# Feature products of an attention layer summed in PSUM by two matmuls of 128 columns, with maxima and exponentials taken straight from PSUM

## The chip, the cores and the metric

The kernel runs on one core of a Trainium2 chip. The metric is the device time of one execution in microseconds (us). Before the change it is 1089.97 us, the median of three runs (1088.09 to 1090.83).

## The reference

The kernel computes a linear attention with random features, followed by a two-layer network with ELU. Cut to what matters:

```python
q_s, k_s = q * scale, k * scale                   # 8 batches x 8 heads, 576 tokens, 64 wide; scale = 64 ** -0.25
def phi(x):
    proj = einsum('bhsd,md->bhsm', x, omega)      # 128 features
    h = proj - sum(x * x, -1, keepdims=True) / 2
    return exp(h - max(h, -1, keepdims=True)) / sqrt(m)
q_p, k_p = phi(q_s), phi(k_s)
kv, z = einsum('bhsm,bhsd->bhmd', k_p, v), sum(k_p, axis=2)
attn = einsum('bhsm,bhmd->bhsd', q_p, kv) / (einsum('bhsm,bhm->bhs', q_p, z)[..., None] + 1e-6)
x = attn.transpose(0, 2, 1, 3).reshape(4608, 512)
return elu(x @ w_in) @ w_out                      # 512 -> 2048 -> 512
```

The change is inside `phi`.

## The kernel before, in words

Two heads make a pair; 32 pairs are worked on one after the other (`pair`, L653). For each pair the kernel loads k, q and v, projects k to features (`project`, L394), forms kv and z (`kv`, L521), projects q, and finishes the division and the product with kv (`finish`, L558). The result lands in a ring of tokens, from which the network reads blocks of 384 tokens: a first layer (`layer1`, L751: matmuls L764 to L766 into the tile ph) and a second (`layer2`, L789: matmuls L798 to L800 into acc). Each of these products is written as three matmuls of type fp32r on a number's head (rounded to fp32r) and its tail (the rest): head by head, head by tail, tail by head.

`project` has two branches. The first pairs (k of pairs 0 to 6, q of pairs 0 to 7) take the branch `native`, with plain fp32 matmuls (L437), a maximum straight from PSUM (L445) and exponentials straight from PSUM (L404). All later ones, 25 projections of k and 24 of q, take the branch below it, which the change rewrites. There a projection has 9 slots of 128 tokens by 128 features:

- x's own tokens are squared on ScalarE (ACT, L457) and summed on VectorE (DVE, L460) into sq, nine numbers per partition.
- y holds x's head in one half of the 128 partitions and its tail in the other (L469 to L477). om holds omega's head in columns 0 to 127 and omega's tail in columns 128 to 255.
- For each slot one matmul of type fp32r with 256 columns (L488), with y stationary and om moving, gives two products of 128 columns side by side. Five chunks of two slots (the last has one) each take a PSUM bank with the tag "pa", of which there are three.
- ACT reads the second product and makes p2 = sq - product (L497). DVE subtracts p2 from the first product, writes h to SBUF and takes its maximum, in one instruction per slot (L506, which the trace shows with a short second one that reads the accumulator).
- ACT negates the maxima (L410) and takes the exponentials of h in SBUF with them as the bias (L404), one instruction per slot, in groups of four and five slots.

The order of the work is set before anything runs. Every step is entered into a plan (`Plan`, L96) with an engine, a cost in nanoseconds and a due time; `Plan.order` goes through a made-up time line with these costs and starts, on each free engine, the ready step that is due first, if its buffers are free. What comes out is a fixed order of instructions for each engine. On the chip every engine follows its list and waits on semaphores. The plan's cost of a matmul is in `mm` (L264). Batches 2 to 7, the pairs 8 to 31, are spread over the network's steps on earlier tokens, so on TensorE (PE) the matmuls of a projection stand between those of the two layers.

Of the kernel before, what the change touches and what calls it, by code (L numbers as in the profile page):

```python
# [18 lines left out]
P = 128  # L19
# [40 lines left out]
CONV_STEP = -0.51  # L60
CONV2 = 0.84
CONV3 = 70.47


SPLIT = (0, 8, 16)
# [30 lines left out]
class Plan:  # L96
# [19 lines left out]
    def op(self, eng, ns, due, fn, reads=(), writes=(), nbytes=0, alt=None):  # L116
        n = len(self.tasks)
        engs = {eng: (ns, 0.0)}
        for e, *t in alt or ():
            engs[e] = tuple(t)  # L120
        f = fn if alt is not None else lambda e: fn()
        deps, bufs = set(), set()
        for k in reads:
            if k in self.writer:
                deps.add(self.writer[k])
            self.readers.setdefault(k, []).append(n)
        for k in writes:
            if k in self.writer:
                deps.add(self.writer[k])
            deps.update(self.readers.pop(k, ()))  # L130
            self.writer[k] = n
        for k in (*reads, *writes):
            b = k[0] if isinstance(k, tuple) else k
            if isinstance(b, Buf):
                bufs.add(b)
        deps.discard(n)
        for b in bufs:
            b.left += 1
        self.tasks.append((engs, due, f, deps, bufs, nbytes))
# [123 lines left out]

def mm(n, m=1):  # L264

    return m * (n / 2.4 + 2.5)


def act(n, psum=False, ptr=False):
    return (51 if psum else 93) + 0.833 * n + (93 if ptr else 0)  # L270


def dve(n, fast=False):
    return 69 + n / (1.92 if fast else 0.96)
# [7 lines left out]
def performer_elu_kernel(  # L282
# [82 lines left out]
    def native(i, what):  # L365
        return i < NNAT[what]

    def bank(i, early, name):

        tag = early if i < NEARLY else "pa"  # L370
        return Buf(ps, [P, 512], F32, tag, name, dict(pa=3, ph=2).get(tag, 1))
# [22 lines left out]
    def project(i, nm, due):  # L394

        s = st[i]
        x = s["x" + nm]
        h = s["h" + nm] = Buf(sb, [P, NJ, M], F32, "h", f"h{nm}_{i}", 4)
        mx, nb = small("mx" + nm, NJ, f"mx{nm}_{i}"), small("nb" + nm, NJ, f"nb{nm}_{i}")

        def exps(g, js, src, due, reads):
            def f():
                for j in js:
                    nc.scalar.activation(  # L404
                        h()[:, j, :], src(j), AF.Exp, bias=nb()[:, j:j + 1], scale=SCALE
                    )
            op("ACT", len(js) * act(M, native(i, nm), True), due, f, (*reads, (nb, g)), ((h, g),))

        def negate(g, js, due):
            op("ACT", act(4), due, lambda: nc.scalar.mul(nb()[:, js], mx()[:, js], -SCALE), ((mx, g),), ((nb, g),))  # L410

        if native(i, nm):
            for a in range(2):
                def square(e, a=a):
                    if e == "ACT":
                        nc.scalar.activation(x()[D:P, a], x()[0:D, a], AF.Square)
                    else:
                        tt(e, x()[D:P, a], x()[0:D, a], x()[0:D, a], ALU.mult)

                op(  # L420
                    "ACT", act(S), due - 3 + a, square, ((x, a),), ((x, a, 2),),
                    alt=other("sq", "POOL", pool(S), "DVE", dve(S)),
                )
            for g in range(3):
                d = due + 2.2 * g
                p = bank(i, "acc%d" % g, f"pp{nm}_{i}_{g}")
                n = 4 if g < 2 else 1
                js = slice(4 * g, 4 * g + n)

                def mms(g=g, p=p):  # L430
                    for c in range(4 if g < 2 else 2):
                        t, a = 2 * g + c // 2, c % 2
                        if g < 2:
                            o = p()[:, c * M:(c + 1) * M]
                        else:
                            o = p()[a * D:a * D + D, 0:M]
                        nc.tensor.matmul(o, x()[:, a, t * P:min(t * P + P, S)], of, start=True, stop=True)  # L437

                def view(p=p):
                    return p().rearrange("p (j x) -> p j x", j=4)  # L440

                op("PE", 872 if g < 2 else 240, d, mms, [*((x, a, 2) for a in range(2)), "of"], (p,))
                op(
                    "DVE", 66 + n * 133, d + 1,
                    lambda js=js, n=n, view=view: nc.vector.tensor_reduce(mx()[:, js], view()[:, 0:n], AX.X, ALU.max),  # L445
                    (p,), ((mx, g),),
                )
                negate(g, js, d + 1.1)
                exps(g, range(js.start, js.stop), lambda j, g=g, view=view: view()[:, j - 4 * g], d + 1.5, (p,))
            return  # L450

        def t():
            return x()[:, 1].rearrange("p (j d) -> p j d", d=D)

        op(
            "ACT", act(S), due - 4,
            lambda: nc.scalar.activation(t(), t(), AF.Square, scale=(SCALE * 0.5) ** 0.5), ((x, 3),), ((x, 3),),  # L457
        )
        sq = small("sq" + nm, NJ, f"sq{nm}_{i}")
        op("DVE", dve(S), due - 3, lambda: nc.vector.tensor_reduce(sq(), t(), AX.X, ALU.add), ((x, 3),), (sq,))  # L460

        y = Buf(sb, [P, 2 * S], F32R, "t", f"t{nm}_{i}", 2)
        for a in range(2):
            r, o = slice(a * D, a * D + D), slice(D - a * D, P - a * D)
            cs = slice(a * S, a * S + S)
            parts = ((x, 0),)
            op(  # L469
                "ACT", act(S), due - 5 + a, lambda e, r=r, cs=cs: copy(e, y()[r, cs], x()[r, 0]), parts, ((y, a, "h"),),  # L470
                alt=other("y_hi", "DVE", dve(S, True)),
            )
            op(
                "POOL", pool(S), due - 4 + a,
                lambda e, r=r, o=o, cs=cs: tt(e, y()[o, cs], x()[r, 0], y()[r, cs].bitcast(F32), ALU.subtract),
                (*parts, (y, a, "h")), ((y, a, "l"),), alt=other("y_lo", "DVE", dve(S)),
            )  # L477
        for c in range(5):
            d = due + 1.1 * c
            p = Buf(ps, [P, 512], F32, "pa", f"pp{nm}_{i}_{c}", 3)  # L480
            p2 = Buf(sb, [P, 2, M], F32, "p2", f"p2{nm}_{i}_{c}", 2)
            n = 2 if c < 4 else 1
            g = 0 if c < 2 else 1

            def mms(c=c, p=p, n=n):
                for a in range(n):
                    o = a * (S + D) + c * P
                    nc.tensor.matmul(p()[:, a * 256:(a + 1) * 256], y()[:, o:o + P], om, start=True, stop=True)  # L488

            def view(p=p):  # L490
                return p().rearrange("p (a x) -> p a x", a=2)

            op("PE", mm(256, n), d, mms, [(y, a, z) for a in range(2) for z in "hl"] + ["oh", "om"], (p,))
            def rest(c=c, n=n, p2=p2, view=view):
                for a in range(n):
                    j = 2 * c + a
                    nc.scalar.activation(  # L497
                        p2()[:, a], view()[:, a, M:], AF.Identity, bias=sq()[:, j:j + 1], scale=-1.0
                    )

            op("ACT", n * act(M, True, True), d + 0.5, rest, (p, sq), (p2,))

            def ttr(c=c, n=n, p2=p2, view=view):
                for a in range(n):
                    j = 2 * c + a
                    nc.vector.tensor_tensor_reduce(  # L506
                        out=h()[:, j, :], in0=view()[:, a, 0:M], in1=p2()[:, a, :], scale=1.0, scalar=LOWEST,
                        op0=ALU.subtract, op1=ALU.max, accum_out=mx()[:, j:j + 1],
                    )

            op("DVE", n * 212, d + 1, ttr, (p, p2), ((h, g, c), (mx, g)))
            if c in (1, 4):
                js = range(0, 4) if c == 1 else range(4, NJ)
                negate(g, slice(js.start, js.stop), d + 1.1)
                exps(g, js, lambda j: h()[:, j, :], d + 1.5, [(h, g, e) for e in range(5)])

    def parts_of(i, nm):
        h = st[i]["h" + nm]
        return [(h, g) for g in range(3 if native(i, nm) else 2)]

    def kv(i, due):  # L521

# [35 lines left out]
    def finish(i, due):  # L558
# [15 lines left out]
        for g in range(3):  # L574
# [3 lines left out]
            slots = [(j, j % 2, slice(0, P)) for j in range(4 * g, 4 * g + 4)]  # L578
            if g == 2:
                slots = [(8, a, slice(a * D, a * D + D)) for a in range(2)]  # L580
            hg = (h, g) if native(i, "q") else (h, min(g, 1))

            def dens(slots=slots):
                for j, a, r in slots:
# [365 lines left out]
```

## Time and profile before

| | before |
|---|---|
| median of three runs | 1089.97 us |
| span of the profiled execution | 1090.7 us |
| TensorE's mean granted clock, share of full speed | 0.987 |
| TensorE matmul records | 5971, busy 97% of the span |
| DVE busy, ACT busy, GpSimd (POOL) busy | 58%, 66%, 37% |
| DMA, mean rate | 162 GB/s |

A record of a matmul holds its way through the array too, so records overlap each other: a matmul of 384 columns is shown as 338 to 348 ns long while the next one starts 0.17 us after it. What a matmul costs TensorE is therefore read from the start of one to the start of the next, and not from its length. "PE" are the matmuls, "PEld" the loads of the stationary operand. A plain fp32 matmul shows as two records, each with a weight load of its own; an fp32r matmul shows as one. The rows of a timeline give the start in us, the time to the end of the last record, the engine, the line, the operation, out<-in, the shapes and the number of records.

### The profile page before, as it was taken

To read this page: it belongs to the slowest core of one execution; us is meant where nothing else is said; L and a number is where in the kernel's file an instruction comes from. 1 tells how busy PE (TensorE), PEld (TensorE's weight loads), DVE (VectorE), ACT (ScalarE), POOL (GpSimd) and SP (SyncE) were. 2 spreads that over 40 slices of the span, in tenths; PEclk is the share of its full clock that TensorE was granted. 3 is DMA by queue.
4 is the path that set the end of the run, shared out by engine and by line. 5 is a ranking of instruction groups with operands and counts; after the bars stand their busy time and mean duration, and the time that the engine had idled before them with its cause. 6 is when DMAs were issued, how large, how long until landed. Compare 5 with 4: busy or idle time off the path is not lost.

```text
span 1090.7 us, 19072 instructions
## 1 busy us (share of the span) xinstructions
PE 1060.6 (97%) x5971; PEld 936.8 (86%) x5971; DVE 635.9 (58%) x2403; ACT 724.7 (66%) x2027; POOL 404.4 (37%) x372
## 2 busy tenths in 40 slices
PE   7979888999999999999999999999999999999998
PEld 7867777889988888999888888899888888899987
DVE  6788988775776775225676666324566775322221
ACT  6878774546988986337888988326888888432222
POOL 3568746661223343222343233322233342222221
PEclk8889998999999999999999999999999999999999
DMA  7554656656663554434554645434444452343431
GB/s 213 171 181 161 208 188 240 218 186 205 207 205 130 169 170 150 165 118 157 176 155 153 193 139 170 162 119 150 162 155 167 157 164 79 117 164 119 161 121 63
DMA packets 53235, 176.90 MB, mean 162 GB/s; under 512 B 6032, under 2 KB 6224, under 8 KB 53136
## 3 DMA queue, kind: packets, MB, share of 16 engines
q1 hardware_dynamic: 53136, 175.69, 48.4%
q8 instruction: 48, 0.79, 0.3%
q14 instruction: 51, 0.42, 0.1%
HBM read 155.48 MB, written 20.19 MB: 161 GB/s over the span
## 4 chain that ended last, share of the span: by engine, by line
PE 79%; DVE 9%; ACT 6%; issue 3%; DMA 1%; POOL 1%; SPq 0%; DVEq 0%; POOLq 0%; ACTq 0%
PE ph L764 11%; PE acc L798 10%; PE acc L800 10%; PE ph L766 10%; PE acc L799 10%; PE ph L765 10%; PE pkv L535 4%; PE ppq L488 3%; PE pn L634 3%; PE pt L607 2%; PE ppk L488 2%; ACT hk L404 1%; DVE u_w L697 1%; DVE u_w L704 1%; DVE u_w L709 1%
## 5 line engine op out<-in xcount | busy, mean ns | idle before, releaser
L336 POOL TENSOR_TENSOR g<-e,g 128x384 fp32r<-128x384 f32 x182 | 189.2, 1040 | 547.7 <-DVE g L333 405.9
L764 PE MATMUL ph<-xh,w1c 128*128 128x384 f32 x768 | 267.5, 348 | 6.7 <-DVE e L777 6.2
L766 PE MATMUL ph<-xh,w1c 128*128 128x384 f32 x768 | 259.8, 338 | 0.0
L765 PE MATMUL ph<-xl,w1c 128*128 128x384 f32 x768 | 259.7, 338 | 0.0
L777 DVE SCALAR_TENSOR_TENSOR e<-e,ph 128x384 f32<-128x384 f32 x192 | 105.9, 552 | 237.2 <-ACT e L774 232.8
L798 PE MATMUL acc<-w2h,g 128*128 128x512 f32 x576 | 231.4, 402 | 0.0
L773 ACT ACTIVATE e<-ph 128x384 f32<-128x384 f32 x192 | 93.6, 488 | 206.4 <-PE ph L766 198.4
L800 PE MATMUL acc<-w2h,g 128*128 128x512 f32 x576 | 227.7, 395 | 0.0
L799 PE MATMUL acc<-w2l,g 128*128 128x512 f32 x576 | 227.4, 395 | 0.0
L764 PEld LDWEIGHTS ph<-xh,w1c 128*128 128x128 f32 x768 | 145.6, 190 | 20.1 <-DVE e L777 8.5
L765 PEld LDWEIGHTS ph<-xl,w1c 128*128 128x128 f32 x768 | 145.8, 190 | 7.2
L766 PEld LDWEIGHTS ph<-xh,w1c 128*128 128x128 f32 x768 | 145.4, 189 | 0.3 <-POOL w1c L336 0.3
L800 PEld LDWEIGHTS acc<-w2h,g 128*128 128x128 f32 x576 | 108.5, 188 | 25.5
L798 PEld LDWEIGHTS acc<-w2h,g 128*128 128x128 f32 x576 | 108.7, 189 | 15.1 <-issue 2.3
L799 PEld LDWEIGHTS acc<-w2l,g 128*128 128x128 f32 x576 | 108.8, 189 | 12.2
L336 POOL TENSOR_TENSOR hq<-hq,den 128x512 f32<-128x512 f32 (+1 forms) x96 | 90.4, 961 | 36.1 <-DVE den L595 24.6
L774 ACT ACTIVATE e<-e 128x384 f32<-128x384 f32 x192 | 100.7, 525 | 3.1
L333 DVE CAST g<-e 128x384 fp32r<-128x384 f32 x166 | 72.8, 439 | 23.5 <-PE acc L800 18.8
L586 DVE CUSTOM_DVE_ANT_0 junk<-hq,pz 128x128 f32<-128x128 f32 (+1 forms) x320 | 74.1, 279 | 16.9 <-PE pz L570 16.1
L506 DVE CUSTOM_DVE_ANT_0 hq<-ppq,p2q 128x128 f32<-128x128 f32 x216 | 54.3, 287 | 41.8 <-ACT p2q L497 40.2
L506 DVE CUSTOM_DVE_ANT_0 hk<-ppk,p2k 128x128 f32<-128x128 f32 x225 | 56.5, 286 | 36.1 <-ACT p2k L497 34.3
L497 ACT ACTIVATE p2q<-ppq,sqq 128x128 f32<-128x128 f32 x216 | 67.8, 367 | 12.5 <-PE ppq L488 10.8
(82 smaller groups left out, 1620.3 us busy)
## 6 DMA issues: line engine op xcount, KB each, us to landing
w1c<-w1s SPq DMA_DIRECT2D x176, 512.0 KB, 3.3
raw_w<-in_w_dram SPq DMA_DIRECT2D x32, 512.0 KB, 3.6
xk<-in_kx_dram SPq DMA_DIRECT2D x25, 576.0 KB, 3.9
xq<-in_qx_dram SPq DMA_DIRECT2D x24, 576.0 KB, 4.6
v<-in_v_dram SPq DMA_DIRECT2D x32, 325.0 KB, 3.4
out_dram<-o SPq DMA_DIRECT2D x36, 256.0 KB, 2.9
w1s<-w1c SPq DMA_DIRECT2D x16, 512.0 KB, 3.2
xq<-in_q_dram SPq DMA_DIRECT2D x8, 288.0 KB, 4.0
```

Source lines behind the costliest of these rows:

```text
L336: (nc.vector if e == "DVE" else nc.gpsimd).tensor_tensor(*args)
L506: nc.vector.tensor_tensor_reduce(out=h()[:, j, :], in0=view()[:, a, 0:M], in1=p2()[:, a, :], scale=1.0, scalar=LOWEST, op0=ALU.subtract, o ...
L586: nc.vector.tensor_tensor_reduce(out=junk()[r], in0=h()[r, j, :], in1=pz()[r, a * P:(a + 1) * P], scale=1.0, scalar=EPS, op0=ALU.mult, op1 ...
L764: nc.tensor.matmul(ph(), wh, xh[:, c, o:o + TB], start=(c == 0), stop=False)
L765: nc.tensor.matmul(ph(), wh, xl[:, c, o:o + TB], start=False, stop=False)
L766: nc.tensor.matmul(ph(), wl, xh[:, c, o:o + TB], start=False, stop=(c == NC - 1))
L773: op("ACT", act(TB, True), due, lambda: nc.scalar.activation(e(), ph(), AF.Relu, scale=-1.0), (p,), (e,))
L774: op("ACT", act(TB), due + 0.2, lambda: nc.scalar.activation(e(), e(), AF.Exp, scale=-1.0), (e,), (e,))
L777: lambda: nc.vector.scalar_tensor_tensor(e(), e(), -1.0, ph(), ALU.add, ALU.max), (p, e), (e,),
L798: nc.tensor.matmul(a(), g()[:, 0, ts], w2h[:, f], start=(f == f0), stop=False)
L799: nc.tensor.matmul(a(), g()[:, 0, ts], w2l[:, f], start=False, stop=False)
L800: nc.tensor.matmul(a(), g()[:, 1, ts], w2h[:, f], start=False, stop=(f == f1 - 1))
```

## The change

In the second branch of `project` the two products of a slot are no longer written side by side but added up in the same 128 columns of PSUM by two matmuls of 128 columns, one with omega's head and one with its tail as the moving operand, both with the same stationary y. Four slots share a bank, so a projection has three groups (4, 4 and 1 slots). The maximum of a group is one DVE instruction on PSUM. sq, which now carries the square of the scale, goes into the bias by two small DVE instructions per group, and the exponentials read PSUM. p2, the ACT steps L497 and L410 of this branch and the DVE step L506 are gone. The divisor in the plan's cost of a matmul gets a name with its value unchanged.

```diff
-            op("ACT", len(js) * act(M, native(i, nm), True), due, f, (*reads, (nb, g)), ((h, g),))
+            op("ACT", len(js) * act(M, True, True), due, f, (*reads, (nb, g)), ((h, g),))
...
-            lambda: nc.scalar.activation(t(), t(), AF.Square, scale=(SCALE * 0.5) ** 0.5), ((x, 3),), ((x, 3),),
+            lambda: nc.scalar.activation(t(), t(), AF.Square, scale=SCALE * 0.5**0.5), ((x, 3),), ((x, 3),),
...
+        def bias(g, js, due):
+            def f():
+                nc.vector.scalar_tensor_tensor(mx()[:, js], mx()[:, js], SCALE, sq()[:, js], ALU.mult, ALU.subtract)
+                nc.vector.scalar_tensor_tensor(nb()[:, js], mx()[:, js], -1.0, sq()[:, js], ALU.mult, ALU.subtract)
+            op("DVE", 2 * dve(4), due, f, ((mx, g), sq), ((mx, g), (nb, g)))
...
-        for c in range(5):
-            p = Buf(ps, [P, 512], F32, "pa", f"pp{nm}_{i}_{c}", 3)
-            n = 2 if c < 4 else 1
...
-                    nc.tensor.matmul(p()[:, a * 256:(a + 1) * 256], y()[:, o:o + P], om, start=True, stop=True)
...
-                    nc.scalar.activation(
-                        p2()[:, a], view()[:, a, M:], AF.Identity, bias=sq()[:, j:j + 1], scale=-1.0
-                    )
...
-                    nc.vector.tensor_tensor_reduce(
-                        out=h()[:, j, :], in0=view()[:, a, 0:M], in1=p2()[:, a, :], scale=1.0, scalar=LOWEST,
-                        op0=ALU.subtract, op1=ALU.max, accum_out=mx()[:, j:j + 1],
-                    )
...
-                negate(g, slice(js.start, js.stop), d + 1.1)
-                exps(g, js, lambda j: h()[:, j, :], d + 1.5, [(h, g, e) for e in range(5)])
+        for g in range(3):
+            p = bank(i, "acc%d" % g, f"pp{nm}_{i}_{g}")
+            n = 4 if g < 2 else 1
...
+                for c in range(n):
+                    o = (c % 2) * (S + D) + (2 * g + c // 2) * P
+                    for m in range(2):
+                        nc.tensor.matmul(
+                            p()[:, c * M:(c + 1) * M], y()[:, o:o + P], om[:, m * M:(m + 1) * M],
+                            start=(m == 0), stop=(m == 1),
+                        )
...
+            op("PE", mm(M, 2 * n), d, mms, [(y, a, z) for a in range(2) for z in "hl"] + ["oh", "om"], (p,))
+            op(
+                "DVE", 66 + n * 133, d + 1,
+                lambda js=js, n=n, view=view: nc.vector.tensor_reduce(mx()[:, js], view()[:, 0:n], AX.X, ALU.max),
+                (p,), ((mx, g),),
+            )
+            bias(g, js, d + 1.1)
+            exps(g, range(js.start, js.stop), lambda j, g=g, view=view: view()[:, j - 4 * g], d + 1.5, (p,))
```

The plan then writes another order. The first place is TensorE at the projection of q for pair 16, in the middle of the program (ppq_16_0 is the bank of its first chunk, tq_16 is y, ph_79 and acc_4 belong to the network). Before:

```order
L488 MATMUL ppq_16_0_5778<-om_73,tq_16_5047 128x256 x2
L764 MATMUL ph_79_5774<-xh_81,w1c_79_5657 128x384
L765 MATMUL ph_79_5774<-xl_82,w1c_79_5657 128x384
L766 MATMUL ph_79_5774<-xh_81,w1c_79_5657 128x384
L535 MATMUL pkv_16_5763<-v_16_4636,hk_16_5629 128x65 x4
L764 MATMUL ph_79_5774<-xh_81,w1c_79_5657 128x384
L765 MATMUL ph_79_5774<-xl_82,w1c_79_5657 128x384
L766 MATMUL ph_79_5774<-xh_81,w1c_79_5657 128x384
L488 MATMUL ppq_16_1_5803<-om_73,tq_16_5047 128x256 x2
```

The same place on TensorE in the changed kernel, where the matmuls of the projection are L496:

```order
L496 MATMUL ppq_16_0_5616<-om_73,tq_16_4888 128x128 x8
L760 MATMUL ph_79_5612<-xh_81,w1c_79_5506 128x384
L761 MATMUL ph_79_5612<-xl_82,w1c_79_5506 128x384
L762 MATMUL ph_79_5612<-xh_81,w1c_79_5506 128x384
L531 MATMUL pkv_16_5601<-v_16_4518,hk_16_5482 128x65 x4
```

Where pieces of two matmuls of 256 columns stood apart, there are pieces of eight matmuls of 128 columns; the work around them is the same.

The second place is ScalarE in the same stretch. Before (p2q is p2, nbq the negated maxima, hq the features, e and kvf belong to other steps):

```order
L497 ACTIVATE p2q_16_0_5784<-ppq_16_0_5778,sqq_16_4922 128x128 x2
L331 COPY kvf0_75<-pkv_16_5763 128x128
L497 ACTIVATE p2q_16_1_5809<-ppq_16_1_5803,sqq_16_4922 128x128 x2
L773 ACTIVATE e_79_5817<-ph_79_5774 128x384
L774 ACTIVATE e_79_5817<-e_79_5817 128x384
L410 ACTIVATE nbq_16_5828<-mxq_16_5792 128x4
L497 ACTIVATE p2q_16_2_5830<-ppq_16_2_5821,sqq_16_4922 128x128 x2
L404 ACTIVATE hq_16_5791<-hq_16_5791,nbq_16_5828 128x128 x4
L497 ACTIVATE p2q_16_3_5857<-ppq_16_3_5834,sqq_16_4922 128x128 x2
L497 ACTIVATE p2q_16_4_5864<-ppq_16_4_5846,sqq_16_4922 128x128
```

The same place on ScalarE in the changed kernel, where the exponentials are L407:

```order
L407 ACTIVATE hq_16_5637<-ppq_16_0_5616,nbq_16_5635 128x128 x4
L334 COPY kvf0_75<-pkv_16_5601 128x128
L769 ACTIVATE e_79_5658<-ph_79_5612 128x384
L770 ACTIVATE e_79_5658<-e_79_5658 128x384
L407 ACTIVATE hq_16_5637<-ppq_16_1_5660,nbq_16_5635 128x128 x4
```

The steps that made p2 and the negated maxima are gone, and the exponentials take the banks of TensorE as their input.

More of the change, by code (lines that the diff above doesn't have):

```diff
@@ L62 @@
 CONV3 = 70.47
+PACE = 2.4
 SPLIT = (0, 8, 16)
@@ L264, in mm @@
 def mm(n, m=1):
-    return m * (n / 2.4 + 2.5)
+    return m * (n / PACE + 2.5)
 def act(n, psum=False, ptr=False):
@@ L477, in project @@
             )
-        for c in range(5):
-            d = due + 1.1 * c
-            p = Buf(ps, [P, 512], F32, "pa", f"pp{nm}_{i}_{c}", 3)
-            p2 = Buf(sb, [P, 2, M], F32, "p2", f"p2{nm}_{i}_{c}", 2)
-            n = 2 if c < 4 else 1
[L483 to L488, printed above, removed]
-            def view(p=p):
[L491 to L497, printed above, removed]
-                        p2()[:, a], view()[:, a, M:], AF.Identity, bias=sq()[:, j:j + 1], scale=-1.0
-                    )
[L501 to L506, printed above, removed]
-                        out=h()[:, j, :], in0=view()[:, a, 0:M], in1=p2()[:, a, :], scale=1.0, scalar=LOWEST,
-                        op0=ALU.subtract, op1=ALU.max, accum_out=mx()[:, j:j + 1],
-                    )
-            op("DVE", n * 212, d + 1, ttr, (p, p2), ((h, g, c), (mx, g)))
-            if c in (1, 4):
-                js = range(0, 4) if c == 1 else range(4, NJ)
-                negate(g, slice(js.start, js.stop), d + 1.1)
-                exps(g, js, lambda j: h()[:, j, :], d + 1.5, [(h, g, e) for e in range(5)])
@@ new lines, in project, with mms @@
+        for g in range(3):
+            d = due + 2.2 * g
+            p = bank(i, "acc%d" % g, f"pp{nm}_{i}_{g}")
+            n = 4 if g < 2 else 1
+            js = slice(4 * g, 4 * g + n)
+            def mms(g=g, n=n, p=p):
+                for c in range(n):
[5 more added lines that the diff above has]
+                        )
+            def view(p=p):
+                return p().rearrange("p (j x) -> p j x", j=4)
+            op("PE", mm(M, 2 * n), d, mms, [(y, a, z) for a in range(2) for z in "hl"] + ["oh", "om"], (p,))
[6 more added lines that the diff above has]
+            exps(g, range(js.start, js.stop), lambda j, g=g, view=view: view()[:, j - 4 * g], d + 1.5, (p,))
@@ L517, in parts_of @@
     def parts_of(i, nm):
         h = st[i]["h" + nm]
-        return [(h, g) for g in range(3 if native(i, nm) else 2)]
+        return [(h, g) for g in range(3)]
     def kv(i, due):
@@ L580, in finish @@
                 slots = [(8, a, slice(a * D, a * D + D)) for a in range(2)]
-            hg = (h, g) if native(i, "q") else (h, min(g, 1))
+            hg = (h, g)
             def dens(slots=slots):
```

## The prediction

> **What bounds the kernel now.** I read first the page's busy times, then the busy times by stage, then the waits of TensorE in the longest stage, and last the timeline of TensorE at a projection. The page's first part:
>
> ```profile
> PE 1060.6 (97%) x5971; PEld 936.8 (86%) x5971; DVE 635.9 (58%) x2403; ACT 724.7 (66%) x2027; POOL 404.4 (37%) x372
> ```
>
> TensorE is the fullest engine. As the share is an average, the stages come next: start and end in us, their length, then busy time and instructions of PE, PEld, DVE, ACT and POOL, the granted clock, DMA share and GB/s.
>
> ```profile
> 58.00:275.00 217.00, 199.69 (x1094) 173.54 (x1095) 173.83 (x405) 142.59 (x369) 130.69 (x102) 0.97 0.58 200
> 275.00:900.00 625.00, 623.58 (x3581) 553.41 (x3579) 365.96 (x1656) 467.14 (x1348) 198.94 (x193) 1.00 0.49 160
> 900.00:1090.00 190.00, 187.02 (x973) 166.41 (x972) 53.45 (x192) 70.61 (x171) 47.33 (x48) 1.00 0.35 118
> ```
>
> From 275 to 900 us TensorE is without work for 625.00 - 623.58 = 1.4 us, while DVE has 259 us free and ACT 158 us. All that the trace shows of TensorE waiting for another engine there (us in total, times, longest) is:
>
> ```profile
> PE pt L607 <- ACT kvf L331: 0.8, 1, 0.8
> PE pt L607 <- POOL hq L336: 0.4, 2, 0.2
> PE pt L607 <- DVE mxq L506: 0.3, 1, 0.3
> ```
>
> No projection waits. From 58 to 275 us TensorE stands still for 217.00 - 199.69 = 17.3 us; DVE is busy for 80% of that stage, with the conversion of the weights. Where the changed matmuls lie in these stages, by the busy times of line L488 alone (PE, PEld):
>
> ```profile
> 0.00:160.00 160.00, 3.69 (x18) 2.98 (x18) 0.94 0.58 185
> 160.00:275.00 115.00, 5.44 (x27) 4.73 (x27) 0.97 0.62 215
> 275.00:900.00 625.00, 79.35 (x371) 64.69 (x371) 1.00 0.49 160
> 900.00:1090.00 190.00, 5.36 (x25) 4.29 (x25) 1.00 0.35 118
> ```
>
> Of 441 slots 396, nine in ten, lie where TensorE has no time left. So the change is worth what it does to TensorE there, and nearly nothing that it saves on ACT or DVE there can shorten the span.
>
> **What a projection costs TensorE before and after.** The timeline of TensorE around 412 us, with the start of each piece and the number of its records at the end:
>
> ```profile
> 411.48 1.00 PE L535 MATMUL pkv<-v,hk 128*128 128x65 f32 x8
> 412.31 0.61 PE L607 MATMUL pt<-ident,hq 128*128 128x128 f32 x4
> 412.68 0.42 PE L764 MATMUL ph<-xh,w1c 128*128 128x384 f32 x1
> ...
> 413.29 0.41 PE L488 MATMUL ppq<-om,tq 128*128 128x256 f32 x2
> 413.53 0.34 PE L764 MATMUL ph<-xh,w1c 128*128 128x384 f32 x1
> 413.71 0.34 PE L765 MATMUL ph<-xl,w1c 128*128 128x384 f32 x1
> 413.89 0.34 PE L766 MATMUL ph<-xh,w1c 128*128 128x384 f32 x1
> ```
>
> Before: two matmuls of 256 columns take 413.53 - 413.29 = 0.24 us from start to start, 0.12 us each, so the nine of a projection take 9 x 0.12 = 1.08 us. 384 columns take 0.18 us (413.53 to 413.71): the time goes with the columns at 256 and 384.
>
> After: 18 matmuls of 128 columns with the same number of column passes. If columns were all, the sum would not change. But each matmul brings a load of its stationary operand, and the first rows below show that the program drops no load where the operand stays the same: L764 and L765 both have w1c's head stationary, one right behind the other, and each has its own 768 loads.
>
> ```profile
> L765 PEld LDWEIGHTS ph<-xl,w1c 128*128 128x128 f32 x768 | 145.8, 190 | 7.2
> L764 PEld LDWEIGHTS ph<-xh,w1c 128*128 128x128 f32 x768 | 145.6, 190 | 20.1 <-DVE e L777 8.5 <-issue 2.5 <-DVE den L586 0.9
> ```
>
> The trace has no fp32r matmul under 256 columns. The nearest rows with a short stream behind a full load are those of plain fp32, above all L535: eight records, each with 65 columns and a load of 128x128, take 412.31 - 411.48 = 0.83 us, 0.104 us each. The same type with 128 columns, L437:
>
> ```profile
> 90.71 1.05 PE L437 MATMUL ppq<-of,xq 128*128 128x128 f32 x8
> 91.60 0.39 PE L530 MATMUL pkv<-v,hk 128*128 128x130 f32 x2
> ```
>
> Eight records take 91.60 - 90.71 = 0.89 us, 0.111 us each. Half the columns save 0.007 us: the short records wait for something that doesn't go with the columns, and I take it to be the load, a floor of about 0.1 us per matmul. A matmul of 256 columns (0.12 us) covers it; one of 128 columns, 0.06 us by its columns, doesn't. A piece of eight short matmuls between longer ones is just what the change makes of four slots, so I take L535's price: 18 x 0.104 = 1.87 us for a projection, 0.79 us more than before. Ends: the four transposes L607, one record each with 128 columns, take 412.68 - 412.31 = 0.37 us, 0.093 us each, which gives 18 x 0.093 = 1.67, +0.59; 0.12 us each (no cheaper than 256 columns) gives 2.16, +1.08.
>
> The Trainium skill, "TensorE: Matmul & The Clock Gate", section LDWEIGHTS, gives a load of P columns P / 1.2 ns, which speaks against this change: 107 ns for 128 columns. By that figure the estimate would be 18 x 0.107 = 1.93 us for a projection, against 1.87 by the row.
>
> By stage: 275 to 900 us holds 371 / 9 = 41.2 projections, x 0.79 = +32.6 us, all on the path. 900 to 1090 us: 25 / 9 = 2.8, +2.2 us, on the path as well. 58 to 275 us: 45 / 9 = 5.0, 4.0 us, of which I count half, since TensorE has gaps there: +2.0. Sum +36.8 us.
>
> **What ACT and DVE save.** Rows by form (busy us, mean ns, idle before):
>
> ```profile
> L497 ACT ACTIVATE p2k<-ppk,sqk 128x128 f32<-128x128 f32 x225 | 68.3, 364 | 8.1 <-PE ppk L488 7.2 <-DVE mxk L506 0.7
> L497 ACT ACTIVATE p2q<-ppq,sqq 128x128 f32<-128x128 f32 x216 | 67.8, 367 | 12.5 <-PE ppq L488 10.8 <-ACT p2q L497 1.3
> L410 ACT ACTIVATE nbk<-mxk 128x5 f32<-128x5 f32 x25 | 5.2, 209 | 2.1 <-DVE mxk L506 2.0
> L404 ACT ACTIVATE hk<-hk,nbk 128x128 f32<-128x128 f32 x225 | 71.4, 397 | 0.5
> L404 ACT ACTIVATE hk<-ppk,nbk 128x128 f32<-128x128 f32 x63 | 18.3, 376 | 0.1
> L506 DVE CUSTOM_DVE_ANT_0 hk<-ppk,p2k 128x128 f32<-128x128 f32 x225 | 56.5, 286 | 36.1 <-ACT p2k L497 34.3
> L506 DVE DVE_READ_ACCUMULATOR2_ANT mxk<- 128x1 f32 x225 | 18.5, 82 | 0.0
> L445 DVE TENSOR_REDUCE mxk<-ppk 128x4 f32<-128x512 f32 x14 | 9.6, 685 | 2.3 <-PE ppk L437 2.2
> L595 DVE RECIPROCAL den<-den 128x4 f32<-128x4 f32 x64 | 10.3, 169 | 0.3
> ```
>
> ACT loses 9 x 0.365 us (p2) and 2 x 0.21 us (negation) per projection, 3.7 us, and its exponentials cost the same from PSUM (376 against 397 ns). DVE loses 9 x (0.286 + 0.082) = 3.3 us and gains two maxima over four slots, one over one slot (0.28 us, as for one slot of L506) and six steps on at most four numbers; the trace has no such step, the nearest is the reciprocal, 0.169 us: 2 x 0.685 + 0.28 + 6 x 0.169 = 2.7 us. DVE is nearly where it was. From 275 to 900 us this buys nothing, for no work waits there that TensorE could take up. From 58 to 275 us five projections take 18 us off ACT and 3 us off DVE; the 17.3 us of TensorE's gaps there hang on DVE and the conversion more than on ACT. I take -3 us, between 0 and -6.
>
> The new wait is that the exponentials hold a bank of TensorE until they end, behind the maximum and two small DVE steps. Now the bank filled at 413.29 us is held like this:
>
> ```profile
> 415.22 0.61 ACT L497 ACTIVATE p2q<-ppq,sqq 128x128 f32<-128x128 f32 x2
> ...
> 417.04 1.27 ACT L404 ACTIVATE hq<-hq,nbq 128x128 f32<-128x128 f32 x4
> 416.02 0.28 DVE L506 CUSTOM_DVE_ANT_0 hq<-ppq,p2q 128x128 f32<-128x128 f32 x1
> ```
>
> The second L506 follows the first at once, so the bank is free at about 416.5 us, 3.2 us after it was filled, and a projection needs five: 16 us. After: 0.83 (matmuls) + 0.69 (maximum) + 2 x 0.17 + 1.27 (four exponentials) = 3.1 us of bare work, and with the 1.7 us that ACT took to come to the bank above (413.53 to 415.22) 4.8 us, twice, and some 3 us for the last slot: 13 us on the same three banks. So I cost the bank at nothing; its cover is that no projection waits now. The new scale of the square and the name of the divisor change no instruction's size. SP issues the same loads and stores, and POOL has the same work but for a few steps that the plan hands to or takes from DVE.
>
> Sum: +36.8 - 3 = +34 us. The span of the profiled execution, 1090.7 us, is 0.7 us over the median and inside the three runs, so I add to the median: 1090.0 + 34 = 1124 us. With the two ends of the load's price, 0.59 x 46.5 - 6 = +21 and 1.08 x 49 = +53 us (46.5 counts half of the early five projections, 49 all): 1111 to 1143 us. Chance 0.66.
>
> **The rivals.**
>
> *The load hides (not slower).* If TensorE loads weights under a stream of 128 columns as it does under 256, a matmul costs half of 0.12 us, 18 x 0.06 = 1.08 us, nothing changes on TensorE, and what is left is the relief of 0 to -6 us: 1087 us, 1084 to 1090. It decides below (1.08 + 3 / 46.5) / 18 = 0.064 us per matmul. For it: columns alone set the price at 256 and 384. Against it: L535's 0.104 us with 65 columns. Chance 0.09, of which 0.05 gain more than 3.3 us (0.3% of the time, about what a measurement of this kernel can tell from no change).
>
> *Pairs of load and matmul run closer than in L535.* L535's matmuls are plain fp32, two records each; one fp32r record might cost less, between 0.06 and 0.093 us. In the middle, 0.08 us: 18 x 0.08 = 1.44, +0.36, x 46.5 - 3 = +14 us: 1104 us. Chance 0.08. The same page of the Trainium skill, section "Back-to-back issue gap", has a stream of loads and matmuls of 128 columns at about 81 ns per matmul, an estimate of 1105 us here; the trace's rows of that width stand above it, though they are of another type.
>
> *A narrow fp32r matmul is no cheaper than a plain fp32 one.* By the rows of L437 a plain matmul of 128 columns, two records, takes 0.89 / 4 = 0.223 us: 18 x 0.223 = 4.01 us, +2.93 us x 49 - 3 = +140 us, 1230 us. Against it: at 256 columns fp32r (L488) shows one record and half the time of L437 for twice the columns, and nothing in the rows makes a type's price depend on its width. For it: no row is as narrow. Chance 0.13.
>
> *The banks hold TensorE up.* If each of the 98 groups of four slots made TensorE wait a quarter of a microsecond for its bank, +24 us on top: 1148 us. Against it is the sum above. Chance 0.04.
>
> **How the numbers follow.** The likeliest case gives 1124 us. The range from 1084 to 1146 us holds it (0.65 of its 0.66), the closer pairs (0.08) and the hidden load (0.08): 0.81; what is left out is nearly all the plain-fp32 price and the banks. Faster by over 0.3%: 0.05; within 0.3%: 0.04, the rest of the hidden load; slower: 0.91.
>
> **What would show it.** In the changed profile a piece of eight of the new matmuls between two of the network should take about 0.83 us from its start to the next start; 0.5 would be the hidden load, 1.8 the plain-fp32 price. PEld's busy time should grow by 441 loads of 0.19 us, 84 us, ACT's should fall by about 180 us, DVE's by some 30, and the span should hardly follow either. The waits of TensorE from 275 to 900 us should stay under a few us, with none of a projection for ACT; a row of that kind would be the banks. The stage that ends with the 371 slots should be longer by 30 to 35 us. The forecast is wrong if the pieces of eight take under 0.6 us, or if TensorE has idle time that it hasn't now.

## The result and the profile after

The changed kernel takes 1133.31 us, median of four runs (1131.17 to 1135.73); the kernel before, run beside it, 1089.6 us. The ratio is 1.040, with a 95% interval from 1.038 to 1.0425: slower by 44 us, where 34 us were forecast. The span of the profiled execution is 1131.3 us, 40.6 us more than before.

The first part of the page of the changed kernel:

```profile
PE 1100.7 (97%) x6412; PEld 977.4 (86%) x6412; DVE 645.1 (57%) x1953; ACT 597.6 (53%) x1494; POOL 402.5 (36%) x375
```

TensorE has 441 more matmuls and 441 more loads, one more per slot. ACT lost 127 us of work, and the kernel became slower. The stages of the changed kernel (columns as before, with the first stage from 0):

```profile
0.00:275.00 275.00, 248.13 (x1456) 215.43 (x1457) 219.00 (x518) 176.26 (x462) 162.49 (x133) 0.96 0.60 197
275.00:900.00 625.00, 624.84 (x3725) 558.64 (x3724) 347.92 (x1181) 335.60 (x834) 179.33 (x181) 1.00 0.46 151
900.00:1132.00 232.00, 227.75 (x1235) 203.29 (x1234) 78.21 (x256) 85.69 (x198) 60.64 (x61) 1.00 0.37 123
```

and the same stages of the kernel before, of which the second stands in the prediction:

```profile
0.00:275.00 275.00, 249.98 (x1421) 216.99 (x1422) 216.48 (x556) 186.96 (x511) 158.15 (x131) 0.95 0.59 197
```

Up to 275 us the changed kernel got through 35 more matmuls in the same time; some five of the 49 projections are done by then, which have 43 matmuls more, so the other work stands 8 matmuls behind, under 2 us. Behind 275 us it had 6412 - 1456 = 4956 matmuls where the kernel before had 5971 - 1421 = 4550: 406 more, in 1131.3 - 275 = 856.3 us where there were 815.7. All of the 40.6 us lie there, 0.100 us for each matmul that was added. TensorE stayed full: from 275 us to the end the waits of TensorE that the trace of the changed kernel shows are one row,

```profile
PE pt L603 <- issue: 0.2, 1, 0.2
```

so neither a bank nor ACT nor DVE holds it up. What it does longer is seen in its timeline at a projection of the changed kernel:

```profile
411.31 0.40 PE L796 MATMUL acc<-w2h,g 128*128 128x512 f32 x1
411.54 1.01 PE L496 MATMUL ppk<-om,tk 128*128 128x128 f32 x8
412.38 0.45 PE L794 MATMUL acc<-w2h,g 128*128 128x512 f32 x1
412.67 0.39 PE L795 MATMUL acc<-w2l,g 128*128 128x512 f32 x1
412.90 0.40 PE L796 MATMUL acc<-w2h,g 128*128 128x512 f32 x1
...
413.65 0.34 PE L496 MATMUL ppk<-om,tk 128*128 128x128 f32 x2
413.82 0.39 PE L760 MATMUL ph<-xh,w1c 128*128 128x384 f32 x1
414.05 0.34 PE L761 MATMUL ph<-xl,w1c 128*128 128x384 f32 x1
```

Eight matmuls of 128 columns take 412.38 - 411.54 = 0.84 us from their start to the next start, as forecast (0.83). But the matmul of 512 columns behind them takes 412.67 - 412.38 = 0.29 us, and the one after that 0.23 us, as such a matmul does elsewhere. Behind the piece of two it is the same: 414.05 - 413.82 = 0.23 us for 384 columns that take 0.17 or 0.18 us elsewhere. Each piece leaves 0.05 to 0.06 us behind it that stands under the line of another matmul. With it the eight cost 0.84 + 0.055 = 0.895 us, 0.112 us each, and a projection 18 x 0.112 = 2.02 us.

### The profile page after: what moved, and what is told of

It is laid out like the page before. It is cut to its first block, busy times and chain, and to the rows that moved or that the text cites. A ratio compares the mean times of both kernels' runs of the same rounds, so it can differ in the third digit from the quotient of the medians.

```text
span 1131.3 us, 18655 instructions
## 1 busy us (share of the span) xinstructions
PE 1100.7 (97%) x6412; PEld 977.4 (86%) x6412; DVE 645.1 (57%) x1953; ACT 597.6 (53%) x1494; POOL 402.5 (36%) x375
## 4 chain that ended last, share of the span: by engine, by line
PE 85%; DVE 6%; ACT 3%; DMA 2%; issue 2%; POOL 1%; SPq 0%; DVEq 0%; POOLq 0%; ACTq 0%
PE acc L794 11%; PE ph L760 11%; PE acc L796 11%; PE acc L795 11%; PE ph L762 11%; PE ph L761 11%; PE pkv L531 5%; PE ppq L496 4%; PE ppk L496 4%; PE pn L630 3%; PE pt L603 2%; DVE u_w L693 1%; DVE u_w L700 1%; PE ppq L440 1%; PE pkv L526 1%
## 5 line engine op out<-in xcount | busy, mean ns | idle before, releaser
L339 POOL TENSOR_TENSOR g<-e,g 128x384 fp32r<-128x384 f32 x181 | 186.0, 1027 | 560.6 <-DVE g L336 452.5
L407 ACT ACTIVATE hk<-ppk,nbk 128x128 f32<-128x128 f32 x288 | 84.2, 373 | 54.2 <-DVE nbk L468 51.3
L407 ACT ACTIVATE hq<-ppq,nbq 128x128 f32<-128x128 f32 x288 | 84.5, 373 | 47.2 <-DVE nbq L468 44.2
L339 POOL TENSOR_TENSOR hq<-hq,den 128x512 f32<-128x512 f32 (+1 forms) x96 | 84.2, 895 | 33.1 <-DVE den L591 32.9
L507 DVE TENSOR_REDUCE mxq<-ppq 128x4 f32<-128x512 f32 (+1 forms) x72 | 40.0, 556 | 87.6 <-PE ppq L496 87.5
```

The lines of the kernel that those rows point to most:

```text
L339: (nc.vector if e == "DVE" else nc.gpsimd).tensor_tensor(*args)
L407: nc.scalar.activation(h()[:, j, :], src(j), AF.Exp, bias=nb()[:, j:j + 1], scale=SCALE)
```

## The experiments

The load theory says that a matmul of 128 columns costs 0.112 us because the load of 128 stationary columns takes that long, whatever streams. Its rivals: narrow fp32r matmuls stream at half rate (stream rival); the second matmul of a slot waits for the sum of the first (sum rival); a good part of the loss comes from the banks, the order or DVE (rest rival).

**TensorE's part alone.** The kernel before, each matmul of 256 columns split into two:

```diff
-                    nc.tensor.matmul(p()[:, a * 256:(a + 1) * 256], y()[:, o:o + P], om, start=True, stop=True)
+                    for m in range(2):
+                        nc.tensor.matmul(
+                            p()[:, a * 256 + m * M:a * 256 + (m + 1) * M], y()[:, o:o + P], om[:, m * M:(m + 1) * M],
+                            start=True, stop=True,
+                        )
```

> The kernel before, with each matmul of 256 columns split into two of 128 columns that write the same places side by side; nothing is summed in PSUM and ACT and DVE work as before. Load theory (each load of 128 stationary columns takes about 0.112 us in a row, whatever streams behind it): 18 x 0.112 = 2.0 us instead of 1.06 per projection, so 1131 to 1137 us, the whole of the change's loss. Stream rival (fp32r under 256 columns streams at half rate, 0.11 us per 128 columns): the same 1131 to 1137 us. Sum rival (the second matmul of a slot waits for the first one's sum in the same columns): 1090 us. Rest rival (a good part of the 44 us comes from the banks, the order or DVE): 1100 to 1120 us.

Measured: 1134.58 us, ratio 1.040 (1.0364 to 1.0436). The split alone costs what the whole change costs, with all of p2, the negations and the old step of DVE still in place, and with nothing summed in PSUM. The sum rival and the rest rival fall; the stream rival gave the same time and stays for the next run. The split kernel's timeline:

```profile
412.76 1.00 PE L489 MATMUL ppk<-om,tk 128*128 128x128 f32 x8
413.60 0.44 PE L802 MATMUL acc<-w2h,g 128*128 128x512 f32 x1
413.88 0.40 PE L803 MATMUL acc<-w2l,g 128*128 128x512 f32 x1
```

0.84 us for eight, and 0.28 us for the 512 columns behind them: the same figure as in the changed kernel, without a sum.

**As many columns, twice the loads.** The changed kernel, each matmul split again:

```diff
-                    for m in range(2):
-                        nc.tensor.matmul(
-                            p()[:, c * M:(c + 1) * M], y()[:, o:o + P], om[:, m * M:(m + 1) * M],
-                            start=(m == 0), stop=(m == 1),
-                        )
+                    for f in range(0, M, 64):
+                        for m in range(2):
+                            nc.tensor.matmul(
+                                p()[:, c * M + f:c * M + f + 64], y()[:, o:o + P], om[:, m * M + f:m * M + f + 64],
+                                start=(m == 0), stop=(m == 1),
+                            )
```

> The changed kernel, with each matmul of 128 columns split into two of 64: 36 matmuls per projection with as many columns in all as before, and twice the loads. Load theory: 36 x 0.112 = 4.03 us instead of 2.02 per projection, +94 to +99 us, 1227 to 1233 us. Stream rival: the columns are the same, 1130 to 1140 us. Sum rival: 18 waits instead of 9, 1175 to 1180 us.

Measured: 1236.8 us, ratio 1.133 (1.129 to 1.138), about 102 us over the changed kernel, a little above the load theory's 94 to 99 us and far from the stream rival. Its timeline:

```profile
409.55 1.87 PE L497 MATMUL ppk<-om,tk 128*128 128x64 f32 x16
411.25 0.48 PE L795 MATMUL acc<-w2h,g 128*128 128x512 f32 x1
411.57 0.40 PE L796 MATMUL acc<-w2l,g 128*128 128x512 f32 x1
```

Sixteen matmuls of 64 columns take 1.70 us, 0.106 us each, and leave 0.09 us behind (0.32 us for 512 columns): 0.112 us each, with half the columns. The price goes with the loads and not with the columns, and the stream rival falls.

**Half the load, as many columns.** The changed kernel, with the tail's matmul first and with 64 stationary columns; the head's matmul overwrites it, so omega's tail is left out of the result:

```diff
-                    for m in range(2):
-                        nc.tensor.matmul(
-                            p()[:, c * M:(c + 1) * M], y()[:, o:o + P], om[:, m * M:(m + 1) * M],
-                            start=(m == 0), stop=(m == 1),
-                        )
+                    for m, r in ((1, 64), (0, P)):
+                        nc.tensor.matmul(
+                            p()[0:r, c * M:(c + 1) * M], y()[:, o:o + r], om[:, m * M:(m + 1) * M],
+                            start=True, stop=True,
+                        )
```

> The changed kernel, with the matmul of omega's tail put first and given only 64 of the 128 tokens of a slot as its stationary operand (64 columns to load, the same 128 columns to stream); the matmul of omega's head then overwrites it, so the products with omega's tail are left out of the result. Load theory, with a load that goes with the number of stationary columns: 9 x 0.112 + 9 x 0.056 = 1.5 us instead of 2.0 per projection, 1107 to 1113 us. Load theory, with a fixed price per load: 1133 us. Stream rival: 1133 us. Sum rival: nothing is summed, about 1090 us.

Measured: 1118.37 us, ratio 1.0255 (1.0222 to 1.0288), 15 us under the changed kernel: between what the load theory gave and what a fixed price gave. The timeline says why:

```profile
406.18 0.84 PE L496 MATMUL ppk<-om,tk 128*64 128x128 f32 x8
406.86 0.45 PE L794 MATMUL acc<-w2h,g 128*128 128x512 f32 x1
407.15 0.39 PE L795 MATMUL acc<-w2l,g 128*128 128x512 f32 x1
...
410.26 0.34 PE L496 MATMUL ppk<-om,tk 128*64 128x128 f32 x2
410.44 0.39 PE L760 MATMUL ph<-xh,w1c 128*128 128x384 f32 x1
```

A piece of eight takes 0.68 instead of 0.84 us, 0.16 us less, that is three halved loads of 0.055 us each; the piece of two takes 0.18 us, no less than before. The first load of a piece is small, but it lay under the long matmul ahead of it anyway. So a projection saves 2 x 0.16 = 0.32 us and not 0.5, and 0.32 x 47 = 15 us. The load's time goes with its stationary columns, and my sum for this run had counted a load that was already hidden.

**The two summed matmuls apart.** The changed kernel, with the loops over m and c exchanged:

```diff
-                for c in range(n):
-                    o = (c % 2) * (S + D) + (2 * g + c // 2) * P
-                    for m in range(2):
+                for m in range(2):
+                    for c in range(n):
+                        o = (c % 2) * (S + D) + (2 * g + c // 2) * P
...
-                            start=(m == 0), stop=(m == 1),
+                            start=(m == 0 and c == 0), stop=(m == 1 and c == n - 1),
```

> The changed kernel, with the order inside a group turned: first the products with omega's head for all slots, then those with its tail, so that the two matmuls that are summed stand three others apart, and no y is loaded twice in a row. Load theory: 1131 to 1136 us as in the changed kernel. Sum rival (a matmul waits for the sum of the one before it in the same columns): back to about 1090 us. If a load of the same operand twice in a row were cheaper, this run would be slower than the changed kernel by over 5 us.

Measured: 1132.65 us, ratio 1.0387 (1.0366 to 1.0408), the changed kernel's time. Neither the sum nor the same y twice in a row matters.

**The other parts alone.** The changed kernel without the tail's matmul (omega's tail is left out of the result), everything else as changed:

```diff
-                    for m in range(2):
-                        nc.tensor.matmul(
-                            p()[:, c * M:(c + 1) * M], y()[:, o:o + P], om[:, m * M:(m + 1) * M],
-                            start=(m == 0), stop=(m == 1),
-                        )
+                    nc.tensor.matmul(p()[:, c * M:(c + 1) * M], y()[:, o:o + P], om[:, 0:M], start=True, stop=True)
```

> The changed kernel with the matmul of omega's tail left out, so that a slot has one matmul of 128 columns and one load; the products with the tail are missing from the result, and everything on ACT and DVE is as in the changed kernel. It shows what the change's other parts are worth once TensorE's part is about what it was. Load theory: 9 x 0.112 = 1.0 us per projection against 1.06 and more before, and a relief of 0 to 6 us: 1083 to 1090 us. Rest rival (banks, order, DVE cost something): over 1095 us. If ACT's and DVE's relief were worth more than I counted: under 1080 us.

Measured: 1089.32 us, ratio 0.9984 (0.9969 to 1.0000). With nine loads TensorE takes 9 x 0.112 = 1.01 us per projection, 0.07 us under the 1.08 us of nine matmuls of 256 columns, which is 3 us over all. That is no less than the whole gain of 2 us (0 to 3 us by the interval): freeing ACT of some 130 us is worth nothing that these runs can tell from zero.

**Short matmuls between long ones.** If a load runs ahead under a long stream, single short matmuls should cost only their columns. The changed kernel with a finer plan (the steps of kv and of the two layers are cut into single matmuls in the same way):

```diff
+                    if eng == "PE" and short and self.kinds[n] == "long":
+                        due -= self.WEAVE
...
+            for c in range(n):
+                for m in range(2):
+                    op(
+                        "PE", mm(M), d, lambda c=c, m=m, mms=mms: mms(c, m),
+                        [(y, a, z) for a in range(2) for z in "hl"] + ["oh", "om"], (p,), kind="short",
+                    )
```

> The changed kernel with every matmul of the projections, of kv and of the two layers a step of its own in the plan, and a rule that after a short matmul (128 or 65 columns) a long one (384 or 512 columns) comes next if it is due within 3 us. A load then has a long stream to hide under. Load theory, with the next load able to run under a long stream: a short matmul between long ones costs about 0.058 us, 18 x 0.058 = 1.04 us per projection, -44 us; a matmul of kv (two records) costs 0.17 instead of 0.22 us, 8 x 0.054 x 26 pairs = -11 us; together 1078 us, between 1072 and 1086. A fixed price of 0.112 us per matmul, whatever its neighbours: 1133 us. If the finer order makes TensorE wait for other engines, in between, with waits in the trace.

Measured: 1135.46 us, ratio 1.0405 (1.0386 to 1.0423). Nothing is gained, though the order is as meant:

```profile
411.42 0.22 PE L502 MATMUL ppk<-om,tk 128*128 128x128 f32 x1
411.48 0.45 PE L803 MATMUL acc<-w2h,g 128*128 128x512 f32 x1
411.77 0.22 PE L502 MATMUL ppk<-om,tk 128*128 128x128 f32 x1
411.82 0.45 PE L803 MATMUL acc<-w2l,g 128*128 128x512 f32 x1
412.11 0.22 PE L502 MATMUL ppk<-om,tk 128*128 128x128 f32 x1
```

A short and a long matmul take 0.34 to 0.35 us together (411.42, 411.77, 412.11), which is 0.23 + 0.112. By the starts the short one has only 0.06 us, but the long one then has 0.29. So a load doesn't run far ahead. No run shows the moment at which a load begins; what fits the times is that the load for the long matmul begins when the short one begins and takes its 0.112 us, with only the short stream of 0.06 us over it; the long stream that comes later hides the next load, no more. The price of a matmul is then the longer of two things, its own stream and the load for the matmul behind it. My forecast for this run had let the load run ahead under any long stream, and that was wrong. The rule fits the run with half the load too: there each of the three matmuls whose next load is halved falls from 0.112 us to about its own stream.

The same plan rule in the kernel before, where only kv has short matmuls:

> The kernel before with the same plan rule; its projections keep their matmuls of 256 columns, which aren't moved by it, and only kv's matmuls of 65 columns count as short. Load theory: -11 us from kv, 1080 us, between 1075 and 1085. A fixed price per matmul: 1090 us.

Measured: 1093.48 us, ratio 1.0012 (0.9999 to 1.0024): no gain. The timeline shows the same reason (L542 is kv's matmul, two records):

```profile
411.58 0.33 PE L542 MATMUL pkv<-v,hk 128*128 128x65 f32 x2
411.73 0.48 PE L805 MATMUL acc<-w2l,g 128*128 128x512 f32 x1
412.04 0.33 PE L542 MATMUL pkv<-v,hk 128*128 128x65 f32 x2
```

One matmul of kv and one of 512 columns take 412.04 - 411.58 = 0.46 us, which is 0.23 + 2 x 0.112.

**The change for the early projections only.** The kernel before, with the changed branch for pairs under 10:

```diff
+        if i < NEW:
+            for g in range(3):
...
+            return
         for c in range(5):
```

> The kernel before, with the changed projection only for the five early ones (k of pairs 7, 8 and 9, q of pairs 8 and 9), which run before 275 us, where TensorE has gaps and ACT and DVE are busy with the weights; the other 44 keep matmuls of 256 columns. One matmul costs the longer of its own stream and the next one's load (0.112 us): the five cost TensorE 5 x 0.94 = 4.7 us more, some of it in gaps, against a relief that I counted at 3 us: 1088 to 1094 us. If the relief in that stage were worth more than TensorE's loss: under 1087 us, and this version would beat both kernels.

Measured: 1094.59 us, ratio 1.0038 (1.0024 to 1.0052). It loses 4 us (2.6 to 5.7 by the interval), at the upper end of what was expected or just above it: also where ACT and DVE are busiest their relief doesn't pay for the loads. The loss is nearly the whole 4.7 us of the loads, so the 3 us of relief did not show.

**The plan told the price.**

```diff
-            op("PE", mm(M, 2 * n), d, mms, [(y, a, z) for a in range(2) for z in "hl"] + ["oh", "om"], (p,))
+            op("PE", 112 * 2 * n, d, mms, [(y, a, z) for a in range(2) for z in "hl"] + ["oh", "om"], (p,))
```

> The changed kernel, with the plan told 112 ns for each of the new matmuls instead of 56, so that its order fits the chip. TensorE's work is the same, and it was without gaps anyway: 1130 to 1135 us. Rest rival (the order made with too low a price costs something): under 1127 us.

Measured: 1145.26 us, ratio 1.0497 (1.0473 to 1.0520), 10 to 12 us slower than the changed kernel (by the ratios and by the medians), against both expectations. The stages from 58 to 160 us and from 160 to 275 us, first of this run:

```profile
58.00:160.00 102.00, 89.88 (x519) 75.20 (x520) 83.36 (x212) 71.28 (x188) 63.86 (x52) 0.90 0.53 174
160.00:275.00 115.00, 107.89 (x544) 96.15 (x542) 87.55 (x132) 51.00 (x107) 67.45 (x51) 0.97 0.56 195
```

and of the changed kernel:

```profile
58.00:160.00 102.00, 90.63 (x546) 76.44 (x547) 89.73 (x231) 75.47 (x200) 69.52 (x54) 0.95 0.57 186
160.00:275.00 115.00, 109.02 (x575) 97.41 (x574) 85.81 (x132) 54.43 (x114) 63.73 (x49) 1.00 0.59 207
```

TensorE is 57 matmuls behind at 275 us (1399 against 1456), with about 2 us more of gaps and a granted clock of 0.90 and 0.97 against 0.95 and 1.00. The clock is the larger part: on average it is 0.94 against 0.98 over these 217 us, which is about 8 us by my estimate. It is lower in all four runs, too: their means over the whole execution are 0.983 to 0.988, the changed kernel's 0.991 to 0.994. The order among the conversions of the weights is another one, but that it causes the gaps or the lower clock was not tried, so the cause stays open. It has no part in the 44 us, since the changed kernel doesn't have this order.

## Why the prediction was right, and where it was off

*What bounds the kernel.* Right. TensorE is without work for 0.2 us from 275 to 900 us (1.4 us before), and all of the added time is TensorE's.

*The load as the floor.* Right, and shown: the time follows the number of loads (twice the loads, about +102 us) and the number of stationary columns (half, -0.16 us in a piece of eight) while the columns that stream are the same. The rivals of a hidden load, of closer pairs and of the plain fp32 price fall with the piece of eight, 0.84 us. That a matmul costs the longer of its own stream and the load for the next one came only with the later runs; the prediction had a floor per matmul, which for pieces of eight comes to the same.

*The price of a projection.* This term of the sum was mis-sized: 18 x 0.104 = 1.87 us, where 18 x 0.112 = 2.02 us was measured. I had taken L535's eight records up to the next start, and what such a piece leaves behind stands under the next matmul's line. In the rows quoted there transposes followed, which were short themselves and hid it. Another place in the trace before, where a long matmul follows, shows it:

```profile
500.52 1.00 PE L535 MATMUL pkv<-v,hk 128*128 128x65 f32 x8
501.33 0.42 PE L764 MATMUL ph<-xh,w1c 128*128 128x384 f32 x1
501.59 0.34 PE L765 MATMUL ph<-xl,w1c 128*128 128x384 f32 x1
```

The eight take 0.81 us, and the 384 columns behind them 0.26 us instead of 0.18: together 0.89 us, 0.111 us each. The transposes, my lower end of 0.093 us, were read short in the same way, as the 384 columns behind them took 0.25 us. My sign of 0.83 us for a piece of eight could not tell the error, since it was read up to the next start as well. So the loss per projection is 2.02 - 1.08 = 0.94 us, and not 0.79: 0.15 x 46.5 = 7 us of the 10 us that were missing in the forecast.

By the Trainium skill, "TensorE: Matmul & The Clock Gate", section LDWEIGHTS, the load of 128 columns takes 107 ns, and 64 columns half of that; the runs agree, with 112 ns and, as an estimate from the 0.055 us saved, about 57 ns. The same page of the Trainium skill, section "Back-to-back issue gap", gives about 81 ns for a matmul of 128 columns in a stream of loads and matmuls; that doesn't hold for fp32r here, where it is 112 ns.

*The relief.* This term, -3 us against +2.0 us of loss in the stage from 58 to 275 us, isn't borne out. The two profiles seem to agree with it, as the changed kernel stood less than 2 us behind at 275 us. But they are one execution each, and the changed kernel's had the higher mean granted clock up to there, 0.96 against 0.95, which by my estimate is worth 2 to 3 us. The run with the change for the early projections only is the better test: -1 us by my two terms, +4 us measured. The run with one matmul per slot agrees, since its gain is no more than that of its cheaper matmuls; it also shows that ACT's relief is worth nothing later. So the remaining 3 us between the forecast and the median may be the relief that didn't come. They may also be scatter: the difference of the spans is 40.6 us, that of the medians 43.7 us. The runs don't settle which.

*The signs.* The 371 slots that lay between 275 and 900 us took 625.1 us before and 661.2 us after, from the 45th slot's last matmul to the 416th's: 36 us more, where I had named 30 to 35. The busy times came out otherwise than I had said. PEld's grew by 41 us and not 84, ACT's fell by 127 us and not 180, and DVE's rose by 9 us where I had it fall by some 30. In part that is because I multiplied counts by the mean length of a record, while records overlap: the 225 records of L497 for k, 364 ns long, fill 68.3 us, which is 304 ns each. The rest was not followed up. None of it changes the forecast's main term.

*The banks.* Costed at nothing, rightly: no row shows TensorE waiting for a bank behind 275 us.

## What to carry to other kernels

On a full TensorE count matmuls before columns: here a matmul of fp32r with 128 or 64 columns cost as much as the load of the next one's stationary operand, so summing in PSUM by two matmuls of 128 columns cost more than one of 256 with the sum made elsewhere. Work taken from engines with time to spare bought nothing while TensorE had none. When a short piece is priced from a timeline, look at the line behind it too, since a part of its cost may stand there.

## What the runs showed of the hardware that I had not expected

Placing a short matmul between two long ones doesn't hide its load: one of 128 and one of 512 columns took 0.34 to 0.35 us together, 0.112 us more than the long one alone, as in a piece of eight. The runs fit a TensorE that loads for the next matmul only, and begins when the current one begins, though no run shows when a load begins.

The recorded starts mislead by about 0.055 us there: the matmul behind a short one starts 0.06 us after it by the record, and pays the rest of the load in its own length (0.45 us instead of 0.39 for 512 columns).
